# A long-convolution and MLP block on one core: ssm_k loaded and transposed in halves, PSUM places in another order, column means and the w2 load moved

## The chip, the core and the metric

The kernel runs on one core of one Trainium2 chip. The metric is the device time of one execution in microseconds (us), the median of several runs; less is better. The engines are named as in the profile: PE (TensorE, matmul), PEld (its weight loads), DVE (VectorE), ACT (ScalarE), POOL (GpSimd), SP (SyncE, which here only issues DMAs).

## The reference

S = 2048 tokens, D = 512 channels, Dff = 1376, batch 1, all inputs bf16.

```
k_shift[t] = sum over j<4 of k[t-j] * shift_k[:, j]        # per channel
kv = k_shift * v
y  = causal convolution of kv with ssm_k along t (by FFT of length 2S) + kv * ssm_D
h  = x + layernorm(x) * y            # x = A_q
h2 = h + relu(layernorm(h) @ w1) @ w2
```

## The kernel before, in words

One function writes the whole program; the schedule is manual, so each engine runs its instructions in the order of the text, and semaphores follow from what tiles are read and written. PSUM has eight banks; pools of it are opened and closed (`push`, `pop`), and a pool that is opened where another was waits for the last readers of what lay there.

The convolution is done as a Fourier transform in two steps, t being split into 32 and 64.

- **Start.** SP loads `sk` (ssm_k, 2 MB, L96), then k and v in four chunks each with transposing DMAs (L107 to L112). ACT issues the small load of `wsh` (L98). DVE and ACT build the tables of sines; `cc_turns` (two DVE instructions, L211 and L181) prepares half of one cosine table, `cc_part` (ACT, L185) finishes it. POOL builds `wdiag` (diagonal matrices of the four taps, L226), the small tables `f1hi`, `f1lo` (L228 to L230), and `f2hi`, `f2lo` (L234), which hold f1 on a block diagonal, then `c2n` (L237).
- **Transposes of ssm_k** (`to_rows`, L260): for each q of 8, eight PE transposes of 128 x 128 into one PSUM bank, then a copy to `kfl` by DVE or ACT in turn.
- **The loop over gb = 0 to 7** (L332): `taps` (L320) does the shifted sum for a chunk of k as eight matmuls into two tap banks and multiplies by v on DVE (L327; the result overwrites `sk`). `stage1` (L267) is the first transform step for 8 channel groups: either four 32-row tiles with f1, or, with `pairs`, two 64-row tiles with f2; its results are copied to `a1k` by ACT and DVE.
- **PSUM places.** `place` (L249) hands out three places of two banks in turn; after the tap banks are given back a fourth is appended (L340).
- **Transposes of kv** (L359 to L371), the second step for the kernel's transform (`ps2k`, L377), stage 1 for kv (L390), then 16 **products** (L408): `stage2` into `u`, a complex product with `kf` on DVE and POOL (L421), and `finish` (L426), which adds the parts on PE (`psy`) and copies back into `kf`. `finish` runs two products behind, the last two after the loop (L457).
- **Inverse.** `inv1` (L547), 16 blocks b, goes from `kf` to `ax` by ACT copies (DVE for b = 4, 9, 14). Between the blocks stand the layer norm of x and the centring of w1: `column_means(n)` (L528, four matmuls into a `pm` bank) for a quarter of w1's columns and a subtraction on DVE (n = 0, 1) or, after a DVE copy, on POOL (n = 2, 3). `inv2` (L606) gives y for half a token quarter in `pz`; `gate` (L596) makes h of it and has it transposed back by an SP DMA. `lift` and `ln1_norm` issue transposing DMAs of x and of its norm on SP.
- **MLP**, four token quarters: `mlp1` (L621, relu on ACT) and `mlp2` (L634). Hooks place the remaining `inv2` halves and two sine tables between its blocks. ACT issues the load of `w2` right after the inverse loop (L589, L591); it lies where `kf` was.

Of the kernel before, what the change touches and what calls it, by code (L numbers as in the profile page):

```python
# [15 lines left out]
P = 128  # L16
# [40 lines left out]
def kernel(  # L57
# [38 lines left out]
    nc.sync.dma_start(out=sk[:], in_=A_ssm_k.rearrange("(c p) t -> p c t", p=P))  # L96
# [120 lines left out]

    f1hi = early.tile([P, 64], BF16, name="f1_hi")
# [9 lines left out]
    nc.gpsimd.tensor_copy(out=f1hi[:, 0:64], in_=f1f[:])  # L228
    nc.gpsimd.tensor_tensor(out=f1f[:], in0=f1f[:], in1=f1hi[:, 0:64], op=ALU.subtract)
    nc.gpsimd.tensor_copy(out=f1lo[:, 0:64], in_=f1f[:])  # L230
# [16 lines left out]
    turn = [0]  # L247

    def place(shape, dtype, name):  # L249
        i = turn[0] % len(places)  # L250
        turn[0] += 1
        return places[i].tile(shape, dtype, tag=f"ps{i}", name=name)
# [7 lines left out]
    def to_rows(src, q, fl, eng):  # L260
        shape = [P, 8, P]
        pst = tap_bank(q % 5 - 3, shape, BF16, "pst") if q % 5 > 2 else place(shape, BF16, "pst")
        for i in range(8):
            nc.tensor.transpose(out=pst[:, i, :], in_=src[:, :, :, 8 * q + i], identity=ident[:])  # L264
        copy(eng, fl[:, :, :, 8 * q:8 * q + 8], pst[:].rearrange("p i (d g) -> p g d i", d=2))

    def stage1(fl, a_out, gb, engs, pairs=False):  # L267

        pss = [bank2("ps1") for _ in range(2)]
        n, tabs = (2, (f2hi, f2lo)) if pairs else (4, (f1hi, f1lo))  # L270
        K = P // n
        for gi in range(8):
            for f in range(2):
                for t in range(n):
                    rows = slice(K * t, K * t + K)
                    if pairs:
                        o = pss[t][:, gi // 4, 128 * (gi % 4):128 * (gi % 4) + 128]
                    else:
                        o = pss[t // 2][:, t % 2, 64 * gi:64 * gi + 64]
                    nc.tensor.matmul(out=o, lhsT=fl[rows, 8 * gb + gi, :, :].rearrange("p d n -> p (d n)"),  # L280
                                     rhs=tabs[f][rows, :], start=(f == 0), stop=(f == 1),
                                     tile_position=(K * t, 0), skip_group_check=True)
        for h in range(2):
            if pairs:
                src = pss[h][:].rearrange("p b (g r c) -> p c (b g) r", g=4, r=2)
            else:
                src = pss[h][:].rearrange("p r (g c) -> p c g r", c=64)
            dst = a_out[:, :, 32 * gb:32 * gb + 32].rearrange("p c (g r) -> p c g r", r=DC)[:, :, :, 2 * h:2 * h + 2]
            for g, eng in enumerate(engs[h]):
                n = 8 // len(engs[h])  # L290
                copy(eng, dst[:, :, g * n:g * n + n], src[:, :, g * n:g * n + n])
# [13 lines left out]
    skv = sk[:].rearrange("p c (a b) -> p c a b", b=64)  # L305
    for q in range(8):
        to_rows(skv, q, kfl, "DADADADA"[q])
    cc_turns(0)
# [23 lines left out]
    for gb in range(8):  # L332
        taps(gb // 2, gb % 2)
        if gb == 0:
            cc_turns(16)
        stage1(kfl, a1k, gb, ("AA", "AD")[gb % 2], pairs=(gb == 2))
# [3 lines left out]
    places.append(pl.push("psX", space=PSUM))  # L340
    for dp, pq in enumerate(halves):
# [48 lines left out]
    for gb in range(8):  # L390
        stage1(xfl, a1x, gb, ("A", "DA" if gb == 4 else "D"), pairs=True)
# [6 lines left out]
    psum = pl.push("psP", bufs=2, space=PSUM)  # L398
# [9 lines left out]
    def product(kp):  # L408
# [3 lines left out]
        for s in range(2):  # L412
            u = psum.tile([P, 2, 256], F32, tag=f"u{s}", name=f"u{s}")
# [12 lines left out]
    def finish(at):  # L426
        kp, (tr, ti) = pending.pop(0)
        for s, (a, b, m) in enumerate(((tr[:, 0], ti[:, 1], ineg), (tr[:, 1], ti[:, 0], ipos))):
            psy = psum.tile([P, 512], F32, tag=f"psy{s}", name=f"psy{s}")
# [26 lines left out]
    load_x(3)  # L456
    while pending:  # L457
        finish(16)
    pl.pop("psP")
# [16 lines left out]
    places[:] = [pl.push("psI", space=PSUM)] * 3  # L476
    turn[0] = 0
    psum1 = pl.push("psC", bufs=2, space=PSUM)
# [46 lines left out]
    FS = 344  # L525
    cen = {}

    def column_means(n):  # L528
        cen[n] = psum1.tile([P, 512], F32, tag="pm", name="pm")
        for c in range(DC):  # L530
            nc.tensor.matmul(out=cen[n][:, 0:FS], lhsT=ones[:], rhs=w1[:, c, n * FS:(n + 1) * FS],
                             start=(c == 0), stop=(c == DC - 1))

# [6 lines left out]

    ec_turns(0)
    ln1_stats(0)
    ec_turns(1)
    column_means(0)
    column_means(1)
# [14 lines left out]
    for b in range(16):  # L560
# [14 lines left out]
        if b == 13:  # L575
            column_means(3)
        if b in (11, 14):
            n = 2 + (b - 11) // 3
            nc.vector.tensor_copy(out=wm[:, n - 2, :], in_=cen[n][:, 0:FS])
            center(nc.gpsimd, n, wm[:, n - 2, :])  # L580
# [7 lines left out]
    nfull = DFF // P  # L588
    nc.scalar.dma_start(out=w2[:, 0:nfull, :], in_=B_w2[0:nfull * P, :].rearrange("(c p) d -> p c d", p=P))  # L589
    if DFF % P:  # L590
        nc.scalar.dma_start(out=w2[0:DFF % P, nfull, :], in_=B_w2[nfull * P:DFF, :])  # L591
# [65 lines left out]

    pl.pop("psC")
    pl.pop("psI")
# [13 lines left out]

    def in_mlp1_0(fc):
        if fc in (6, 8):
            ec_sins(2 + (fc - 6) // 2)
# [68 lines left out]
```

## Time and profile before

| | us |
|---|---|
| median of 3 runs (216.83 to 219.06) | 218.42 |
| the profiled execution, its own time | 216.73 |
| its span in the profile | 215.0 |
| PE busy | 195.1 (91%) |
| DVE, ACT, POOL busy | 144.2, 116.6, 79.6 |
| `sk` load, issue to landing | 8.2 |
| 64 transposes of `sk` (L264), busy | 6.5 |
| MLP matmuls (L628 and L645), busy | 78.2 |

The granted PE clock is 0.998 of full speed over the whole span. The DMA engines moved 20.06 MB; the transposing DMAs on SP's queue make up most of the packets. In the table and below, a start is counted from the span's start. A group line of the profile gives line, engine, operation, what is written and read, the count, busy time, the mean of one, and the idle time ahead of it with what ended it.

### The profile page before, as it was taken

The numbers are of one execution on the slowest core, as the hardware profiler recorded it, in microseconds if no ns is written. First come the engines' busy times: TensorE is split into PE (matmuls) and PEld (weight loads), VectorE is DVE, ScalarE is ACT, GpSimd is POOL, SyncE is SP. The second block draws the span as 40 slices with busy tenths as digits, with TensorE's granted clock in tenths as the row PEclk, the third lists the DMA queues.
The fourth block names the chain that finished last, engine by engine and source line by source line (L and its number), as shares of the span: only waits on it lengthen the run. The fifth ranks groups of instructions, "written<-read, shape, count | busy, mean of one in ns | idle before, by whom it ended". The sixth has DMA issues, their size and how long they took to land.

```text
span 215.0 us, 5414 instructions
## 1 busy us (share of the span) xinstructions
PE 195.1 (91%) x2235; PEld 137.3 (64%) x2235; DVE 144.2 (67%) x238; ACT 116.6 (54%) x178; POOL 79.6 (37%) x120
## 2 busy tenths in 40 slices
PE   0398998999996999998997999999999999999992
PEld 0394554999875899986997954664646644444451
DVE  7589778776796999988495993968395460243031
ACT  2967788655796788883996048202450047016400
POOL 3299993000003999995747702200201010002000
PEclk9999999999999999999999999999999999999999
DMA  6999960000000007709850897787353430020012
GB/s 192 314 219 182 159 137 6 2 2 3 0 3 5 0 3 195 262 8 212 173 98 3 265 168 129 88 184 100 76 105 68 92 82 0 15 63 23 0 50 49
DMA packets 49512, 20.06 MB, mean 93 GB/s; under 512 B 44400, under 2 KB 47952, under 8 KB 49488
## 3 DMA queue, kind: packets, MB, share of 16 engines
q1 hardware_dynamic: 47360, 18.24, 42.8%
q10 hardware_dynamic: 2128, 1.48, 2.3%
q8 instruction: 17, 0.28, 0.6%
q14 instruction: 7, 0.06, 0.1%
HBM read 7.08 MB, written 2.10 MB: 43 GB/s over the span
## 4 chain that ended last, share of the span: by engine, by line
PE 79%; DVE 7%; ACT 5%; DMA 5%; issue 1%; SPq 0%; ACTq 0%
PE ps2m L645 18%; PE ps1m L628 18%; PE pz L616 7%; PE pkv L324 6%; PE psy L431 6%; DMA sk<-in_A_ssm_k_dram 4%; PE ps L280 4%; PE ps2k L300 3%; PE ps2k L298 3%; PE u L298 3%; PE u L300 3%; PE pst L264 3%; PE psi L552 3%; ACT ax L242 2%; PE pst L362 2%; ACT a1x L242 2%
## 5 line engine op out<-in xcount | busy, mean ns | idle before, releaser
L630 ACT ACTIVATE h1T<-ps1m 128x512 bf16<-128x512 f32 (+1 forms) x44 | 26.0, 596 | 55.6 <-PE ps1m L628 55.6
L645 PE MATMUL ps2m<-w,h1T 128*128 128x512 bf16 (+3 forms) x187 | 39.4, 367 | 0.0
L628 PE MATMUL ps1m<-xT,w 128*128 128x512 bf16 (+1 forms) x176 | 38.8, 379 | 0.0
L648 DVE SCALAR_TENSOR_TENSOR o<-ps2m,rstd,xh 128x512 bf16<-128x512 f32 (+1 forms) x17 | 12.2, 719 | 32.1 <-PE ps2m L645 29.8
L628 PEld LDWEIGHTS <-w 128*128 128x128 bf16 (+1 forms) x176 | 17.5, 100 | 20.1
L645 PEld LDWEIGHTS <-h1T 128*128 128x128 bf16 (+1 forms) x187 | 17.9, 98 | 19.2
L421 POOL TENSOR_TENSOR t<-usb,kf 128x320 fp32r<-128x320 f32 x32 | 28.2, 930 | 2.4 <-ACT usb L417 2.0
L421 DVE TENSOR_TENSOR t<-u,kf 128x704 fp32r<-128x704 f32 x32 | 26.7, 889 | 3.4 <-ACT usb L417 3.4
L502 POOL TENSOR_SCALAR rstd<-mv 128x4 f32<-128x4 f32 x8 | 2.3, 283 | 67.6 <-DVE mv L500 67.6
L498 DVE BATCH_NORM_STATS2 st<-xh 128x6 f32<-128x512 bf16 x32 | 19.7, 678 | 0.0
L242 ACT CAST kf<-psy 128x512 fp32r<-128x512 f32 x30 | 17.6, 645 | 1.9 <-PE psy L431 0.3
L616 PEld LDWEIGHTS pz<-ecore,ax 32*128 32x128 f32 x512 | 15.2, 186 | 3.8 <-issue 2.1
L616 PE MATMUL pz<-ecore,ax 32*128 32x128 f32 (+7 forms) x512 | 16.1, 273 | 1.3 <-ACT ax L242 1.1
L598 DVE TENSOR_TENSOR qT<-pz,qT 128x1024 bf16<-128x1024 f32 x8 | 9.8, 1222 | 10.2 <-PE pz L616 6.7
L324 PE MATMUL pkv<-kT,wdiag 128*128 128x512 bf16 x64 | 15.2, 380 | 0.9 <-DVE sk L327 0.9
L431 PE MATMUL psy<-t,ipos 128*128 128x512 f32 x48 | 16.0, 393 | 0.0
L552 PE MATMUL psi<-dre,kf 128*128 128x256 f32 x64 | 15.5, 286 | 0.0
L552 PE MATMUL psi<-dim,kf 128*128 128x256 f32 x64 | 15.2, 280 | 0.0
L242 ACT CAST a1k<-ps 128x1024 fp32r<-128x1024 f32 x12 | 12.6, 1093 | 4.3 <-PE ps L280 4.3
L242 ACT CAST ax<-psi 128x1024 fp32r<-128x1024 f32 x13 | 12.4, 1017 | 4.6 <-DVE st L498 3.0
L264 PE MATMUL pst<-ident,sk 128*128 128x128 bf16 x64 | 6.5, 285 | 8.9 <-DMA sk<-in_A_ssm_k_dram 8.9
L327 DVE TENSOR_TENSOR sk<-pkv,vT 128x512 bf16<-128x512 f32 x16 | 10.6, 685 | 3.5 <-PE pkv L324 3.5
(116 smaller groups left out, 391.2 us busy)
## 6 DMA issues: line engine op xcount, KB each, us to landing
sk<-in_A_ssm_k_dram SPq DMA_DIRECT2D x1, 2048.0 KB, 8.2
xh<-in_A_q_dram SPq DMA_DIRECT2D x16, 128.0 KB, 3.0
out_dram<-o SPq DMA_DIRECT2D x60, 32.0 KB, 1.6
w<-in_B_w_dram SPq DMA_DIRECT2D x1, 1376.0 KB, 6.1
w<-in_B_w_dram ACTq DMA_DIRECT2D x1, 1280.0 KB
xh<-xT SPq DMA_TRANSPOSE x8, 3.6
w<-in_B_w_dram ACTq DMA_DIRECT2D x1, 96.0 KB, 8.2
kT<-in_A_k_dram SPq DMA_TRANSPOSE x4, 7.2
```

What stands on the lines that cost most here:

```text
L242: nc.scalar.copy(out=o, in_=i)
L264: nc.tensor.transpose(out=pst[:, i, :], in_=src[:, :, :, 8 * q + i], identity=ident[:])
L298: nc.tensor.matmul(out=ps[:, kk, :], lhsT=at_k1(w_re, k1), rhs=a_in[:, k1, :], start=True, stop=False, skip_group_check=True)
L324: nc.tensor.matmul(out=pss[i][:], lhsT=wdiag[:, 2 * h + i, j, :], rhs=kT[c][:, 2 * h + i, 16 - j:CH + 16 - j], start=(j == 0), stop=(j == ...
L421: eng.tensor_tensor(out=t[:, :, j, :], in0=in0.unsqueeze(1).to_broadcast([P, 2, n, 2]), in1=kfr[:, :, j, ks], op=ALU.mult)
L431: nc.tensor.matmul(out=psy[:], lhsT=m_[:], rhs=t_.rearrange("p j k -> p (j k)"), start=first, stop=not first)
L498: nc.vector.bn_stats(out=st[:, i, :], in_=src[:, i, :])
L552: nc.tensor.matmul(out=ps[:, i // 2, i % 2, :], lhsT=kf[:, c, 4 * m:4 * m + 4, :].rearrange("p r k -> p (r k)"), rhs=d[:].rearrange("p d a ...
L616: nc.tensor.matmul(out=pz[:, rg, 32 * jl:32 * (jl + w)], lhsT=ax[rows, 64 * rho + n2, :, :].rearrange("p d g -> p (d g)"), rhs=ecore[q][ro ...
L628: nc.tensor.matmul(out=ps1[:fsz, :].rearrange("p (i t) -> p i t", i=4), lhsT=w1[:, c, fc * P:fc * P + fsz], rhs=hT[sc][:, :, c, :], start= ...
L630: nc.scalar.activation(out=h1T[:fsz, fc, :], in_=ps1[:fsz, :], func=ACT.Relu)
L645: nc.tensor.matmul(out=ps2[:, 0:w], lhsT=h1T[:ksz, fc, i * P:(i + 1) * P], rhs=w2[:ksz, fc, ds], start=(fc == 0), stop=(fc == NFC - 1))
```

## The change

`sk` comes in two loads of two channel blocks each. Its transposes are 128 instead of 64, each of 64 columns into one half of the PSUM partitions: all of the first half, then all of the second, in eight banks at once; the eight copies follow. `cc_turns(0)` is issued ahead of the copies and `cc_turns(16)` after the taps of group 2 instead of group 0. Stage 1 takes its small tables from the f2 tiles in every group; in the first stage 1 groups 2, 3 and 4 are in 64-row form (before: 2), in the second all but group 0 (before: all). POOL makes `f1hi` and `f1lo` between the second and the third `wdiag`. The places follow a list that is set to 1, 3, 2, 0 once the fourth exists. The products' PSUM pool is split in two (`psU`, `psY`); the mean banks and one place of the inverse stage are opened where `psU` was, the first two column means come right after the last product, and the fourth leaves the loop over b for its end. `w2` is loaded from the hook of the first `mlp1` after its second relu.

```diff
     sk = early.tile([P, DC, S], BF16, name="sk")
-    nc.sync.dma_start(out=sk[:], in_=A_ssm_k.rearrange("(c p) t -> p c t", p=P))
+    for c in range(2):
+        nc.sync.dma_start(out=sk[:, 2 * c:2 * c + 2, :], in_=A_ssm_k[2 * c * P:2 * c * P + 2 * P, :].rearrange("(c p) t -> p c t", p=P))
     wsh = consts.tile([P, DC, KS], BF16, name="wsh")
...
 
+    cc_turns(0)
+
     f1hi = early.tile([P, 64], BF16, name="f1_hi")
...
                                 in1=wsh[:, rg, :].unsqueeze(2).to_broadcast([P, KS, P]), op=ALU.mult)
-    nc.gpsimd.tensor_copy(out=f1hi[:, 0:64], in_=f1f[:])
-    nc.gpsimd.tensor_tensor(out=f1f[:], in0=f1f[:], in1=f1hi[:, 0:64], op=ALU.subtract)
-    nc.gpsimd.tensor_copy(out=f1lo[:, 0:64], in_=f1f[:])
+        if rg == 1:
+            nc.gpsimd.tensor_copy(out=f1hi[:, 0:64], in_=f1f[:])
+            nc.gpsimd.tensor_tensor(out=f1f[:], in0=f1f[:], in1=f1hi[:, 0:64], op=ALU.subtract)
+            nc.gpsimd.tensor_copy(out=f1lo[:, 0:64], in_=f1f[:])
     for f, g in ((f1hi, f2hi), (f1lo, f2lo)):
...
     places = [psum] * 3
-    turn = [0]
+    ring = [0, 1, 2]
 
     def place(shape, dtype, name):
-        i = turn[0] % len(places)
-        turn[0] += 1
+        i = ring.pop(0)
+        ring.append(i)
         return places[i].tile(shape, dtype, tag=f"ps{i}", name=name)
...
 
-    def to_rows(src, q, fl, eng):
-        shape = [P, 8, P]
-        pst = tap_bank(q % 5 - 3, shape, BF16, "pst") if q % 5 > 2 else place(shape, BF16, "pst")
-        for i in range(8):
-            nc.tensor.transpose(out=pst[:, i, :], in_=src[:, :, :, 8 * q + i], identity=ident[:])
-        copy(eng, fl[:, :, :, 8 * q:8 * q + 8], pst[:].rearrange("p i (d g) -> p g d i", d=2))
-
     def stage1(fl, a_out, gb, engs, pairs=False):
...
         pss = [bank2("ps1") for _ in range(2)]
-        n, tabs = (2, (f2hi, f2lo)) if pairs else (4, (f1hi, f1lo))
+        n, tabs = 2 if pairs else 4, (f2hi, f2lo)
         K = P // n
...
                     rows = slice(K * t, K * t + K)
+                    cols = slice(0, P)
                     if pairs:
...
                     else:
+                        cols = slice(64 * (t % 2), 64 * (t % 2) + 64)
                         o = pss[t // 2][:, t % 2, 64 * gi:64 * gi + 64]
                     nc.tensor.matmul(out=o, lhsT=fl[rows, 8 * gb + gi, :, :].rearrange("p d n -> p (d n)"),
-                                     rhs=tabs[f][rows, :], start=(f == 0), stop=(f == 1),
+                                     rhs=tabs[f][rows, cols], start=(f == 0), stop=(f == 1),
                                      tile_position=(K * t, 0), skip_group_check=True)
...
     skv = sk[:].rearrange("p c (a b) -> p c a b", b=64)
+    psts = [tap_bank(i, [P, 8, P], BF16, "pst")[:] for i in range(2)]
+    for i in range(3):
+        pair = place([P, 2, 8, P], BF16, "pst")
+        psts += [pair[:, 0], pair[:, 1]]
+    for h, rows in enumerate(halves):
+        for q in range(8):
+            for i in range(8):
+                nc.tensor.transpose(out=psts[q][rows, i, :], in_=skv[:, 2 * h:2 * h + 2, :, 8 * q + i], identity=ident[:],
+                                    tile_position=(0, 64 * h))
     for q in range(8):
-        to_rows(skv, q, kfl, "DADADADA"[q])
-    cc_turns(0)
+        copy("DA"[q % 2], kfl[:, :, :, 8 * q:8 * q + 8], psts[q].rearrange("p i (d g) -> p g d i", d=2))
     dre = consts.tile([P, 2, 2, 64], F32R, name="dre")
...
         taps(gb // 2, gb % 2)
-        if gb == 0:
+        if gb == 2:
             cc_turns(16)
-        stage1(kfl, a1k, gb, ("AA", "AD")[gb % 2], pairs=(gb == 2))
+        stage1(kfl, a1k, gb, ("AA", "AD")[gb % 2], pairs=(1 < gb < 5))
         if gb in (0, 1, 3, 5):
...
     places.append(pl.push("psX", space=PSUM))
+    ring[:] = [1, 3, 2, 0]
     for dp, pq in enumerate(halves):
...
     for gb in range(8):
-        stage1(xfl, a1x, gb, ("A", "DA" if gb == 4 else "D"), pairs=True)
+        stage1(xfl, a1x, gb, ("A", "DA" if gb == 4 else "D"), pairs=(gb > 0))
     pl.pop("psX")
...
     prod = pl.push("prod", bufs=3, side="right")
-    psum = pl.push("psP", bufs=2, space=PSUM)
+    psu = pl.push("psU", bufs=2, space=PSUM)
+    psy_ = pl.push("psY", bufs=2, side="right", space=PSUM)
     ipos = prod.tile([P, P], F32R, name="ipos", bufs=1)
...
         for s in range(2):
-            u = psum.tile([P, 2, 256], F32, tag=f"u{s}", name=f"u{s}")
+            u = psu.tile([P, 2, 256], F32, tag=f"u{s}", name=f"u{s}")
             stage2(u, a1x, kp, s)
...
         for s, (a, b, m) in enumerate(((tr[:, 0], ti[:, 1], ineg), (tr[:, 1], ti[:, 0], ipos))):
-            psy = psum.tile([P, 512], F32, tag=f"psy{s}", name=f"psy{s}")
+            psy = psy_.tile([P, 512], F32, tag=f"psy{s}", name=f"psy{s}")
             for m_, t_, first in ((ipos, a, True), (m, b, False)):
...
     load_x(3)
+    pl.pop("psU")
+    psum1 = pl.push("psC", space=PSUM)
+    psum_a = pl.push("psIa", space=PSUM)
+    FS = 344
+    cen = {}
+
+    def column_means(n):
+        cen[n] = psum1.tile([P, 512], F32, tag=f"pm{n % 2}", name="pm")
+        for c in range(DC):
+            nc.tensor.matmul(out=cen[n][:, 0:FS], lhsT=ones[:], rhs=w1[:, c, n * FS:(n + 1) * FS],
+                             start=(c == 0), stop=(c == DC - 1))
+
     while pending:
         finish(16)
-    pl.pop("psP")
+    column_means(0)
+    column_means(1)
+    pl.pop("psY")
+    places[:] = [psum_a] + [pl.push("psIb", side="right", space=PSUM)] * 2
+    ring[:] = [0, 1, 2]
     pl.pop("prod")
...
     act_pool = {0: late, 1: late}
-    places[:] = [pl.push("psI", space=PSUM)] * 3
-    turn[0] = 0
-    psum1 = pl.push("psC", bufs=2, space=PSUM)
 
...
 
-    FS = 344
-    cen = {}
-
-    def column_means(n):
-        cen[n] = psum1.tile([P, 512], F32, tag="pm", name="pm")
-        for c in range(DC):
-            nc.tensor.matmul(out=cen[n][:, 0:FS], lhsT=ones[:], rhs=w1[:, c, n * FS:(n + 1) * FS],
-                             start=(c == 0), stop=(c == DC - 1))
-
     def center(eng, n, mean):
...
 
+    def off_center(n):
+        nc.vector.tensor_copy(out=wm[:, n - 2, :], in_=cen[n][:, 0:FS])
+        center(nc.gpsimd, n, wm[:, n - 2, :])
+
     ec_turns(0)
...
     ec_turns(1)
-    column_means(0)
-    column_means(1)
 
...
             column_means(2)
-        if b == 13:
-            column_means(3)
-        if b in (11, 14):
-            n = 2 + (b - 11) // 3
-            nc.vector.tensor_copy(out=wm[:, n - 2, :], in_=cen[n][:, 0:FS])
-            center(nc.gpsimd, n, wm[:, n - 2, :])
+        if b == 11:
+            off_center(2)
+    column_means(3)
+    off_center(3)
     ln1_stats(1)
...
     w2 = mp.tile([P, NFC, D], BF16, name="w2")
-    nfull = DFF // P
-    nc.scalar.dma_start(out=w2[:, 0:nfull, :], in_=B_w2[0:nfull * P, :].rearrange("(c p) d -> p c d", p=P))
-    if DFF % P:
-        nc.scalar.dma_start(out=w2[0:DFF % P, nfull, :], in_=B_w2[nfull * P:DFF, :])
     hT = {}
...
 
+    pl.pop("psIa")
     pl.pop("psC")
-    pl.pop("psI")
+    pl.pop("psIb")
     psz = pl.push("psZ", space=PSUM)
...
 
+    def load_w2():
+        nfull = DFF // P
+        nc.scalar.dma_start(out=w2[:, 0:nfull, :], in_=B_w2[0:nfull * P, :].rearrange("(c p) d -> p c d", p=P))
+        if DFF % P:
+            nc.scalar.dma_start(out=w2[0:DFF % P, nfull, :], in_=B_w2[nfull * P:DFF, :])
+
     def in_mlp1_0(fc):
+        if fc == 1:
+            load_w2()
         if fc in (6, 8):
...
```

## The prediction

> **What bounds the kernel now.** I read the page first (shares by engine), then the chain of work that ended last, then the timeline of each of the three places that the change touches. PE is busy 91% of the span and 79% of the chain, at a granted clock of 0.998; from 124.5 us to 211 us the chain is PE without a gap, and nothing in the change alters that MLP part except the arrival of `w2`. So a gain can only come from the places ahead of 124.5 us where PE waits. The chain shows them (start us, duration us, what):
>
> ```profile
> 0.72 8.18 DMA sk<-in_A_ssm_k_dram
> 8.95 6.49 PE pst L264 x64
> 15.44 1.74 PE pkv L324 x8
> 17.24 1.28 DVE sk L327 x2
> 18.52 0.61 DVE w_tc L211
> 19.15 1.40 DVE w_tc L181
> 20.55 0.60 DVE sk L327
> 21.20 1.89 PE pkv L324 x8
> ...
> 36.68 1.06 ACT a1k L242
> 37.83 3.88 PE pst L362 x32
> ...
> 114.53 0.60 PE pm L531 x4
> 115.13 1.92 PE psi L552 x16
> 117.07 1.02 ACT ax L242
> 118.14 4.06 PE pz L616 x127
> ```
>
> To be seen: 8.2 us of load with PE idle, then 64 transposes on the path; the two `w_tc` instructions on DVE ahead of a tap product; a wait for an ACT eviction before the second transposes; a column mean inside the inverse stage and 1.1 us of PE waiting for ACT behind it. Two timelines add what the chain hides (POOL at the start; PE after the products):
>
> ```profile
> 9.24 4.06 POOL L226 TENSOR_TENSOR wdiag<-ident,wsh 128x512 bf16<-128x512 bf16 x4 [6.07 <-DMA wsh<-in_A_shift_k_dram]
> 15.26 1.43 POOL L234 COPY f_lo<-f_lo 32x64 bf16<-32x64 bf16 x4
> ```
> ```profile
> 99.20 1.34 PE L531 MATMUL pm<-w,ones 128*128 128x344 bf16 x8 [0.84 <-DVE kf L244]
> ```
>
> POOL starts only when `wsh` lands (9.24) and finishes the padded table `f2lo` at 16.69. The column means wait 0.84 us because every PSUM buffer of the products must be free first.
>
> **What the Trainium skill says.** "TensorEngine Tiling (Array Packing)", Restrictions: column tiling disables Fast Weight Load. "TensorE: Matmul & The Clock Gate", LDWEIGHTS: a load's time goes with its columns, not its rows; the trace agrees on rows (32x128 load 92 ns, 64x128 load 94 ns). The strided 128-column load from `sk` takes 188 ns against 98 for the dense `wdiag`, so it may already be a slow load. "DMA: Bandwidth & Descriptors", Queues, rings and completion order: an engine goes round between its queues packet by packet. From 4 to 5 us the trace has 99 packets on SP's queue and 98 on ACT's, which agrees.
>
> **The change, part by part.**
>
> *Two loads, 128 narrow transposes.* SP issues one more DMA (0.47 us), all behind a running transfer. By the 1 us windows 1.05 MB of `sk` has moved by 5.4 us and all 2.1 MB by 8.05; PE started 0.9 us after that, so half one is usable at 6.3 us. Then 64 transposes of 64 columns start there and 64 more follow. A 128-column pair now costs 6.25/63 = 99 ns. No row shows the narrow one: if its cost goes with the loaded columns it is about 50 ns plus, with the moving 128 columns as the other limit; the two-row-tile stage 1 pairs with the same 128 moving columns take 1.12/16 = 70 ns. If the narrow load costs as much as the wide one it is 99 ns. I take 50 to 70: all transposes end at 6.3 + 128 x 0.06 = 14.0 (13 to 15.3) instead of 15.3; with 99 at 19.0. The evacuations (4 x 1.22 on DVE, 4 x 1.02 on ACT) can begin at about 10.6 and end at about 15.5 (before: 16.5). Taps then end at about 16.
>
> *But stage 1 of group 0 now reads `f2hi` and `f2lo`*, ready at 16.69. Moving the three `f1` instructions (0.8 us) between `wdiag` 1 and 2 changes no sum: POOL still has 4.06 + 0.8 + 2.5 us after 9.24, and `wsh` can't land sooner, as its packets alternate with the same 512 rows of `sk`. Stage 1 so starts at 16.8 instead of 17.10: -0.3, whatever the 2 us of early transposes promise.
>
> *The tap loop.* `cc_turns(0)` (1.4 us) moves into DVE's idle time at 8.1 to 10; `cc_turns(16)` (1.4 to 2.1) goes behind group 2, where DVE has 4.0 us of work in 5.9. PE's two waits for DVE (0.2 and 0.72, at 17.97 and 21.20) go: -0.9. Two more groups in 64-row form cost 1.12 - 0.62 each: +1.0. With ACT a little late for group 2 (its first copies and the 1.27 us table come first) I add 0.3, half of it in parallel: +0.15. Without cover I see nothing that hides the +1.0. The loop ends at 36.5 - 0.3 - 0.9 + 1.0 + 0.15 = 36.45; the sum is about 0 to -0.4, and I use -0.3. The transposed k and v must not be overtaken: the last v chunk is issued at 25.55 and takes 5.4 us (31.0), its user runs at 32.95, so 2 us of lead is all that is left there.
>
> *Free order of PSUM places.* The second transposes start at 37.83 because their first place is the one that ACT evacuates at 36.66 to 37.73. In the order 1, 3, 2, 0 they start when the last tap product is written (36.71): -1.1 there. DVE is busy until 37.93 with the other eviction, so the last four are held: redoing the eight by 0.485 us each, with copies of 0.69 and 1.2, the last ends at 40.7 instead of 41.44: -0.75.
>
> *Group 0 of the x stage in 32-row form.* PE saves 0.5, but the stage is paced by ACT: its last `kf` copy ends at 57.28, and 8 copies of 1.12 and a half follow. 0.
>
> *Means behind the products.* `psC` and the first inverse place lie in the banks of `psU`, whose last reader is done at 97.2; PE goes from the last product (98.36) straight into the 8 mean matmuls (1.04) and the inverse stage starts at 99.45 instead of 100.24, just after DVE's last `kf` write at 99.14: -0.8. `column_means(3)` (0.6) leaves the loop and runs while ACT does its last `ax` copy: the loop ends 1.4 us earlier (115.6), ACT's copy at 116.7, and `pz` starts at 116.8 instead of 118.14: -1.35. Behind the moved mean stand on DVE its 0.5 us copy (116.25 to 116.75), the second statistics (2.8), and both gates (1.9 each): they end at 123.3, where PE's own three `pz` halves end at 123.05. MLP starts at 123.4 instead of 124.5: -1.1. POOL's subtraction (2.84) ends at 119.6, 4 us before its use.
>
> *w2 late.* The two DMAs move from 117.1 to ACT's second relu, 1.95 us after MLP start M. Queued behind them on ACT: relu 2 and on, 0.27 us of idle time in each, and four PSUM buffers; nothing. `w2` is first read at M + 9.5. Before, its second part landed 8.2 us after issue; `w1`, of the same size, 6.1. Uncontended: M + 8.1 to M + 9.8. But SP's transposes of x and q run from M + 1.2 to M + 6 and land at about M + 8.5; alternating with 1 KB packets (50 ns against about 20) stretches the 4.4 us of transfer to 6.2, so M + 10.7 at worst in this count. Wait: 0 to 1.2; I take +0.4, since half of the first transpose is over by then. Cover gone: a late qT delays the gate that the next `pz` half waits for; it has 2.2 us to spare.
>
> **Sum** against the span of 215.0 (216.73 with what lies around it): -0.3 - 0.75 - 1.1 + 0.4 = -1.75, near 215.0 for such an execution. The median shown is 218.42, 1.7 above the profiled one; the same difference gives 216.7. I go to 216.5, since the stage 1 wait may give 0.2 more.
>
> **Rivals.**
> - *w2 stalls PE* (chance 0.20). PE has no other work between the two MLP halves. If the transposes take half of each engine, 1.4 MB needs 8 us: landing at M + 12, wait 2.0 to 2.5 in place of 0.4, and the late gate adds up to 0.6. 216.5 + 2 = 218.5. For it: both queues share 16 engines that are saturated from 126 to 132 (share 1.06). Against: `w1` moved at 340 GB/s alone.
> - *The narrow transposes cost as much as wide ones* (0.12), the slower end. At 99 ns each they end at 19.0, taps at 20.8, stage 1 at 20.9: +3.8 in place of -0.3, so 216.5 + 4.1 = 220.6. It decides from 83 ns: 6.3 + 128 x 0.083 + 1.9 = 18.8 is where the other gains (1.75) are eaten. For it: twice as many instructions on the same columns moved; against: loads go with columns.
> - *More than counted* (0.18): the POOL chain ends sooner, and the tap loop is paced by ACT (18.2 us of copies and tables) so that the 64-row groups cost nothing. Then -1.5 more: 215.0.
>
> **How the numbers follow.** The counted case has 0.50, with its own range 215.4 to 217.8. About 1% (2.2 us) is what a measurement of this kernel can tell from no change. Faster by more (under 216.2): 0.28 of the counted case and the 0.18, together 0.46. Within: 0.22, 0.18 of the w2 rival and 0.03, 0.43. Slower: 0.11. The range leaves out the far half of the slow rival and the best few per cent: 214.0 to 219.6.
>
> **What would show it.** First narrow transpose at 6.3 and last before 15; stage 1's first matmul at POOL's last `f_lo` copy; second transposes one us after the last tap stage without an ACT wait; no gap between products and means; `pz` right behind ACT's last `ax`; MLP start about 2.2 us sooner; at the first `ps2m`, either no wait or one for the `w` DMA. I am wrong if PE waits there for over 1 us, if the transposes pace at over 83 ns, or if POOL is no longer last ahead of stage 1.

## The result, and the profile after

The changed kernel takes 223.90 us (median of 4 runs, 223.60 to 224.41) where the kernel before took 217.79 beside it (4 runs, 216.83 to 219.06): a ratio of 1.028, 95% interval 1.022 to 1.034. The forecast of 216.5 and its range are both missed; the kernel became 6.1 us slower. The profiled execution has a time of 223.77 us and a span of 222.0 (before: 215.0). The ratios, here and below, leave out executions more than 1.5% above the fastest of the same kernel, and the medians don't, so the two need not agree to the last digit.

The same marks on PE in both profiles (the first start of each kind of matmul, in us; the tap loop is taken to the end of its last stage 1 matmul) show where the 7.0 us of span lie:

| stretch | before | after | difference | forecast |
|---|---|---|---|---|
| span's start to first stage 1 matmul | 17.10 | 22.60 | +5.50 | -0.3, with the next row |
| tap loop, first stage 1 matmul to the end of the last | 19.50 | 19.09 | -0.41 | |
| loop's end to first `ps2k` | 4.87 | 3.93 | -0.94 | -0.75 |
| `ps2k` to first `u` | 25.80 | 26.20 | +0.40 | 0 |
| `u` to MLP start | 57.23 | 55.81 | -1.42 | -1.1 |
| MLP start to the `pz` behind the first `ps2m` | 11.97 | 15.45 | +3.48 | +0.4 |
| from there to the span's end | 78.53 | 78.92 | +0.39 | 0 |

So the middle of the kernel did roughly what was forecast, and both ends did not. The chain of work that ended last, after, at the kernel's start:

```profile
0.72 5.42 DMA sk<-in_A_ssm_k_dram
...
6.18 14.07 PE pst L312 x128
...
20.27 1.24 DVE kfl L248
...
21.53 1.02 ACT kfl L246
...
22.60 0.72 PE ps L279 x64
```

The first half of `sk` is usable at 6.18, as forecast (6.3), but the 128 narrow transposes take 14.07 us, 110 ns each, where 64 wide ones took 6.49. Behind them two copies stand one after the other, DVE's and then ACT's; in the kernel before such copies overlapped. The waits of ACT after (total, times, longest) say the same:

```profile
ACT kfl L246 <- DVE kfl L248: 3.6, 3, 2.0
```

POOL, forecast as the last ahead of stage 1, is long done (its timeline after):

```profile
6.45 2.04 POOL L229 TENSOR_TENSOR wdiag<-ident,wsh 128x512 bf16<-128x512 bf16 x2 [3.28 <-DMA wsh<-in_A_shift_k_dram]
14.87 1.09 POOL L238 COPY f_lo<-f_lo 32x64 bf16<-32x64 bf16 x4
```

The timeline of PE after, in the middle: the second transposes follow the tap loop at 0.26 us and wait for DVE, not for ACT's eviction, and the means have no wait ahead of them (before: 0.84).

```profile
41.95 3.88 PE L370 MATMUL pst<-ident,sk 128*128 128x128 f32 x32 [0.26 <-DVE sk L334]
102.73 1.34 PE L475 MATMUL pm<-w,ones 128*128 128x344 bf16 x8
```

At the MLP, the waits of PE after (total, times, longest) and the DMA view's count of packets from 132 to 133 us (then MB and their share of the engines' time; q10 is ACT's queue with `w2`, q1 is SP's with the transposes of x and q):

```profile
PE ps2m L654 <- DMA w<-in_B_w_dram: 2.9, 1, 2.9
PE pz L625 <- DVE qT L607: 0.4, 1, 0.4
```
```profile
q10 hardware_dynamic: 226, 0.23, 79.8%
q1 hardware_dynamic: 232, 0.06, 33.4%
```

PE stands still for 2.9 us until `w2` is there. The two queues share the engines one packet for one packet (226 against 232; in the next two windows of 1 us 275 against 271 and 278 against 285), although a packet of `w2` carries 1 KB and one of the transposes 256 B. ACT issues the load at 129.57; its packets begin at 131.7 and end near 140, and on SP's side the last transpose of q lands 10.8 us after its issue, so the gate and the next `pz` are late too.

Taking turns is not all of it. At 275 packets a microsecond the 1408 packets of `w2` would need 5.1 us, and at the 353 to 370 that they reach alone in e3 (below) about 3.9 (estimates from these counts); they took 8.1. Part of the rest is standstill: between 135.5 and 135.9 and between 137.2 and 138.4 next to no packet starts on either queue, and the packets of `w2` that start at 137.1 take 1.4 us each, against 46 ns at the median. From 137 to 138:

```profile
q10 hardware_dynamic: 42, 0.04, 115.6%
q1 hardware_dynamic: 49, 0.01, 65.0%
```

Packets of over 1.3 us occur on SP's queue in the profile of every kernel here, also where `w2` isn't moving (at 125 us in e5, at 133 in e2 below). What holds the DMA engines then stays open.

### The profile page after: what moved, and what is told of

It reads as the page before. It is cut to its first block, busy times and chain, and to the rows that moved or that the text cites. A ratio compares the mean times of both kernels' runs of the same rounds, so it can differ in the third digit from the quotient of the medians.

```text
span 222.0 us, 5464 instructions
## 1 busy us (share of the span) xinstructions
PE 202.5 (91%) x2253; PEld 145.1 (65%) x2267; DVE 145.2 (65%) x238; ACT 116.1 (52%) x178; POOL 79.4 (36%) x120
## 4 chain that ended last, share of the span: by engine, by line
PE 73%; DVE 10%; DMA 8%; ACT 4%; issue 2%; SPq 1%; DVEq 0%; ACTq 0%
PE ps2m L654 14%; PE ps1m L637 13%; PE psy L440 7%; PE pst L312 6%; PE pkv L331 6%; DMA qT<-qln 5%; PE ps L279 5%; PE pz L625 4%; PE ps2k L297 3%; PE ps2k L299 3%; PE u L297 3%; PE psi L567 3%; PE u L299 3%; DMA sk<-in_A_ssm_k_dram 2%; PE pst L370 2%
## 5 line engine op out<-in xcount | busy, mean ns | idle before, releaser
L654 PE MATMUL ps2m<-w,h1T 128*128 128x512 bf16 (+2 forms) x179 | 38.7, 366 | 3.5 <-DMA w<-in_B_w_dram 2.9
L312 PE MATMUL pst<-ident,sk 128*64 128x128 bf16 x128 | 14.1, 292 | 6.2 <-DMA sk<-in_A_ssm_k_dram 6.2
L312 PEld LDWEIGHTS <-sk 128*64 128x64 bf16 x128 | 13.9, 204 | 6.2 <-DMA sk<-in_A_ssm_k_dram 6.2
## 6 DMA issues: line engine op xcount, KB each, us to landing
w<-in_B_w_dram ACTq DMA_DIRECT2D x1, 1280.0 KB, 10.6
```

The costliest lines, as they stand in the source:

```text
L312: nc.tensor.transpose(out=psts[q][rows, i, :], in_=skv[:, 2 * h:2 * h + 2, :, 8 * q + i], identity=ident[:], tile_position=(0, 64 * h))
L654: nc.tensor.matmul(out=ps2[:, 0:w], lhsT=h1T[:ksz, fc, i * P:(i + 1) * P], rhs=w2[:ksz, fc, ds], start=(fc == 0), stop=(fc == NFC - 1))
```

## Experiments

Times are medians in us; "before" is the kernel before, run beside each on the same chip. The kernel before read between 216.76 and 217.79 in the course of them, so differences from the changed kernel, which was run at another time, carry up to 1 us of that: the 5.8, 3.9 and 7.5 us of e1, e2 and e3 below are 5.5, 3.6 and 7.2 when each kernel is taken against the kernel before beside it. In several of these kernels the executions fall into two groups some 2 us apart, the upper with a granted clock near 0.99, and medians mix them; what lies behind is told with the third experiment.

| kernel | time | before | ratio, 95% interval |
|---|---|---|---|
| changed kernel | 223.90 | 217.79 | 1.028 (1.022 to 1.034) |
| e1, wide transposes | 218.13 | 217.48 | 1.003 (1.001 to 1.006) |
| e2, `w2` early | 220.04 | 217.48 | 1.011 (1.009 to 1.014) |
| e3, both | 216.41 | 217.48 | 0.997 (0.994 to 0.999) |
| e4, before with `w2` late | 219.18 | 216.99 | 1.011 (1.007 to 1.015) |
| e5, e3 with tiles of its own | 216.39 | 216.99 | 0.996 (0.992 to 1.000) |
| e6, e5 with `w2` in two | 214.73 | 216.99 | 0.989 (0.984 to 0.993) |
| e7, alternating transposes | 220.48 | 216.99 | one run |
| e8, e6 with one 64-row group | 216.98 | 217.26 | 0.998 (0.995 to 1.001) |
| e9, e6 with the old place order | 216.07 | 217.26 | 0.996 (0.993 to 0.998) |
| e10, e6 with the fourth mean inside | 215.57 | 217.26 | 0.995 (0.992 to 0.998) |
| e11, e6 once more | 215.26 | 216.76 | 0.993 (0.991 to 0.996) |

**e1: the wide transposes put back.** The two loads, the eight banks and all else stay.

```diff
-    for h, rows in enumerate(halves):
-        for q in range(8):
-            for i in range(8):
-                nc.tensor.transpose(out=psts[q][rows, i, :], in_=skv[:, 2 * h:2 * h + 2, :, 8 * q + i], identity=ident[:],
-                                    tile_position=(0, 64 * h))
+    for q in range(8):
+        for i in range(8):
+            nc.tensor.transpose(out=psts[q][:, i, :], in_=skv[:, :, :, 8 * q + i], identity=ident[:])
```

> The changed kernel with the 128 narrow transposes put back to 64 wide ones (128 columns, into the same eight banks, both loads kept); all else as changed. Theory (each narrow transpose costs as much PE time as a wide one, about 109 ns, so the block takes 14.1 us in place of 6.4): transposes end near 15.3 us instead of 20.25, the first stage 1 moves from 22.6 to about 17.5, and the time falls by 4.5 to 5.5 us, to about 219. Rival (stage 1 of group 0 is held by the padded f2 table on POOL and by the copies of two places that share one tile, not by the transposes): the time falls by less than 2.5 us.

Measured: 5.8 us less than the changed kernel. Stage 1 starts at 17.76 instead of 22.60. The narrow transposes are the larger part of the loss.

**e2: `w2` loaded behind the inverse loop again**, narrow transposes kept.

```diff
     w2 = mp.tile([P, NFC, D], BF16, name="w2")
+    load_w2()
...
-        if fc == 1:
-            load_w2()
```

> The changed kernel with the load of w2 put back behind the inverse loop; all else as changed. Theory (w2 and the transposing DMAs of x and q share the 16 DMA engines packet by packet, so w2 takes 10.6 us to land and the q transpose 10.8; PE waits 2.9 us for the one and about 0.9 for the other): both waits go, the time falls by 3 to 4 us, to about 220.3. Rival (PE would stand at the first ps2m for something else, or the late gate alone sets the pace): it falls by less than 1.5 us.

Measured: 3.9 us less than the changed kernel. PE waits for no DMA at `ps2m`; from the first `ps1m` to the first `ps2m` it takes 9.50 us, as in the kernel before (9.50), where the changed kernel took 12.55.

**e3: both.**

> The changed kernel with both put back: wide transposes and w2 behind the inverse loop. Theory (the two costs are at different places and add; what remains of the change, the order of places and the means behind the products, is worth about 2.3 us): 8 to 9 us less than the changed kernel, about 215.3, 1% less than the kernel before. Rival (the remaining edits are hidden or paid back by the two additional 64-row groups): equal to the kernel before within 0.5%.

Measured: 216.41, 1.1 above the expectation, 7.5 below the changed kernel. Its 20 runs fall into 11 at 215.57 to 216.63 (clock 0.996 and more) and 9 at 217.54 to 219.12 (clock 0.984 to 0.991). The profile caught one of the latter. Its timeline of PE and its 1 us windows (the number after the busy shares is the clock, then the DMA share and GB/s):

```profile
116.19 5.01 PE L630 MATMUL pz<-ecore,ax 32*128 32x256 f32 x162 [0.70 <-DVE wm L553]
123.35 2.07 PE L630 MATMUL pz<-ecore,ax 32*128 32x256 f32 x30 [2.15 <-issue]
```
```profile
122.00:123.00 1.00, 0.00 (x0) 0.00 (x0) 1.00 (x4) 0.00 (x0) 0.00 (x0) 1.00 1.25 182
123.00:124.00 1.00, 0.65 (x12) 0.65 (x16) 1.00 (x5) 0.00 (x0) 0.00 (x0) 0.68 0.47 97
124.00:125.00 1.00, 1.00 (x24) 1.00 (x22) 1.00 (x5) 0.00 (x0) 0.00 (x0) 0.50 1.12 192
125.00:126.00 1.00, 1.00 (x10) 0.41 (x5) 1.00 (x3) 0.00 (x0) 0.00 (x0) 0.50 2.31 159
126.00:127.00 1.00, 1.00 (x4) 0.38 (x3) 1.00 (x3) 0.00 (x0) 0.00 (x0) 0.61 0.13 7
```

PE stands still for 2.15 us with nothing that the profile shows to wait for ("issue"), and then its clock is at half from 123.3 to 126.8. From `pz` to the MLP start it takes 9.17 us, 6.27 in e1, and 0.7 more is lost behind it. That is 3.6 us, more than the 2.2 between the medians of the two groups, so the lower group may hold a part of the stop as well (no profile of it was taken). It accounts for part of the difference between e1's gain and e2's (together 9.6) and e3's (7.5): from the lower group's median, 215.94, e3's gain is 8.0.

**Six orders of transposes**, to price the narrow one: the 128 transposes of the changed kernel are replaced by six runs of 32. In turn: strided columns of 64 in one column tile, consecutive columns of 64 in one column tile, strided with the column tiles in turn, consecutive with the column tiles in turn, strided columns of 128, consecutive columns of 128.

```diff
+    for q in range(4):
+        for i in range(8):
+            nc.tensor.transpose(out=psts[q][lo, i, :], in_=skv[:, 0:2, :, 8 * q + i], identity=ident[:], tile_position=(0, 0))
+    for q in range(4):
+        for i in range(8):
+            nc.tensor.transpose(out=psts[q][lo, i, :], in_=sk[:, i % 4, 64 * (8 * q + i):64 * (8 * q + i) + 64], identity=ident[:], tile_position=(0, 0))
...
```

> A measurement of the transposes by themselves: the block of transposes of the changed kernel is replaced by six runs of 32, one after the other: narrow (64 columns) with a stride of 64 elements in one column tile; narrow and dense in one column tile; narrow strided with the two column tiles in turn; narrow dense in turn; wide strided; wide dense. The output isn't the reference's, since the transposed data are others. Theory A (the load of 64 columns costs what one of 128 does, since the narrow form loads slowly): about 109 ns each in all four narrow runs, 99 for wide strided, less for wide dense. Theory B (inside one column tile the next load waits for the matmul before it): about 109 in one tile, about 55 to 70 in turn. Theory C (the stride is what costs): about 109 strided, under 80 dense, in narrow and wide alike.

Measured in a single execution, of which only this stretch is used, by the timeline of PE:

```profile
6.11 3.79 PE L311 MATMUL pst<-ident,sk 128*64 128x128 bf16 x32 [6.11 <-DMA sk<-in_A_ssm_k_dram]
9.73 1.84 PE L314 MATMUL pst<-ident,sk 128*64 128x128 bf16 x30
...
11.52 2.13 PE L318 MATMUL pst<-ident,sk 128*64 128x128 bf16 x31
13.37 1.17 PE L322 MATMUL pst<-ident,sk 128*64 128x128 bf16 x32
14.47 3.09 PE L325 MATMUL pst<-ident,sk 128*128 128x128 bf16 x32
17.40 1.95 PE L328 MATMUL pst<-ident,sk 128*128 128x128 bf16 x32
19.19 1.03 PE L346 MATMUL pkv<-kT,wdiag 128*128 128x512 bf16 x4
```

From start to start, divided by 32: 113 ns (strided, one column tile), 56 (consecutive), 58 (strided, in turn), 34 (consecutive, in turn), 92 (wide, strided), 56 (wide, consecutive). The two that matter by their weight loads:

```profile
L311 PEld LDWEIGHTS <-sk x32: 187/206/208, 6.1 to 9.6; 128*64 128x64 bf16 x32
L325 PEld LDWEIGHTS <-sk x32: 168/203/217, 14.5 to 17.2; 128*128 128x128 bf16 x32
```

A strided load of 64 columns takes 206 ns at the median, one of 128 columns 203: half the columns save nothing. The stride doubles both (consecutive: 110 and 98). So none of the three theories holds alone: a consecutive narrow load isn't dear (against A), and a strided one is dear only behind another on the same column tile (B and C together). The 50 to 70 ns of the forecast is what consecutive columns cost, or strided ones whose neighbours go to the other column tile.

The clock has to be kept apart from this. The records of the granted clock begin only at 9.7 us in this run, at 12.0 in the changed kernel and at 12.6 in the kernel before; the 0.998 in the table of the kernel before takes the time ahead of them as full speed. At these times the matmuls get shorter (317 to 275 ns in the changed kernel), and the wide transposes of the kernel before go from 107 ns each to 91. The narrow strided ones stay at 110 to 113 ns, and their loads at 203 to 207, on both sides of 12.0. So the first of the six runs, which lies ahead of 9.7, may be compared with the fifth; and the 99 ns that the prediction read for a wide transpose is a mean of 107 and 91, so behind 12 us the narrow form costs 110 to 112 against 91.

**e7: that last point in the kernel.** The loop over the two column tiles becomes the innermost one; every pair then needs both loads.

```diff
-    for h, rows in enumerate(halves):
-        for q in range(8):
-            for i in range(8):
+    for q in range(8):
+        for i in range(8):
+            for h, rows in enumerate(halves):
```

> The changed kernel with the loop over the two column tiles innermost, so that each 64-column transpose is followed by one on the other column tile; all of them now wait for the second load (8.8 us). Theory (a strided 64-column load takes 110 ns behind another on the same column tile, and 65 ns when the column tiles alternate, as in the run with six orders): 128 x 65 ns, so transposes from 8.8 to 17.1 and the first tap at 17.2 instead of 20.2, stage 1 near 20.5 and 1.5 to 2.5 us less than the changed kernel. Rival (a 64-column load simply costs what a 128-column load costs, 99 ns or more): 128 x 99 to 110 ns, transposes until 21.5 to 22.9, 1.3 to 2.7 us slower than the changed kernel.

```profile
6.05 0.37 PE L312 MATMUL pst<-ident,sk 128*64 128x128 bf16 x1 [6.05 <-DMA sk<-in_A_ssm_k_dram]
8.72 8.05 PE L312 MATMUL pst<-ident,sk 128*64 128x128 bf16 x127 [2.30 <-DMA sk<-in_A_ssm_k_dram]
16.70 1.47 PE L331 MATMUL pkv<-kT,wdiag 128*128 128x512 bf16 x5
```

Measured: 63 ns each, the first tap at 16.70 (expected 17.2), 3.4 us less than the changed kernel although all but the first start 2.5 us later. The same 128 instructions in another order take 8.0 us in place of 14.0, so the cost is in two strided loads to one column tile in a row, not in the number of instructions. It is still behind the wide form (15.3). The total is from one execution, in which PE also stopped for 2.18 us ahead of `ps2m` and then ran at half clock; the start of the profile is what counts here.

**e4: the kernel before with `w2` late, and nothing else.** The issue moves from behind the inverse loop into the hook, as in the change's diff.

> The kernel before, with its w2 load alone moved to the second relu of the first MLP. Theory of contention (w2 alternates packet by packet with SP's transposes and so lands 10 to 11 us after its issue, where it lands in 6 when the queues are free): first MLP product at about 124.3, w2 issued at about 126.6, landing at about 137, while the second MLP's product wants it at 134: 3 us of PE wait at ps2m, and 0.4 to 0.7 more from the late q transposes; 3.0 to 3.7 us above before. Rival, as it was forecast: a load off the critical path, a gain of 0.2 against a wait of under 0.6, so 217.4 to 218.2.

Measured: 2.2 us more than before. The large part lands 9.3 us after its issue; first `ps1m` to first `ps2m` takes 11.26 us (before 9.50), from there to the next `pz` 3.07 (2.47): 2.4 together. The wait is there without any other part of the change, so the rival falls; it is 1 us smaller than in the changed kernel, as the load lands 1.3 us sooner, and the expected 3.0 to 3.7 was too much.

The landing time is the cause: the DMA issues of the changed kernel and then of e3 (engine, count, size, median us to landing).

```profile
w<-in_B_w_dram ACTq DMA_DIRECT2D x1, 1280.0 KB, 10.6
```
```profile
w<-in_B_w_dram ACTq DMA_DIRECT2D x1, 1280.0 KB, 6.3
```

With the queues free the load takes 6.3 us here, 6.6 in e2 and 7.8 in e5, and 129.57 + 6.3 to 7.8 = 135.9 to 137.4 would have been ahead of the product's place at 137.1 (127.63 + 9.50) or 0.3 behind it. Beside SP's transposes it takes 9.3 to 10.6 (e4, e1, the changed kernel); its first packet then starts 2.0 to 2.1 us after the issue, not 1.05.

**e5: one PSUM tile for each eight transposes**, on top of e3: `to_rows` of the kernel before comes back.

```diff
-    psts = [tap_bank(i, [P, 8, P], BF16, "pst")[:] for i in range(2)]
-    for i in range(3):
-        pair = place([P, 2, 8, P], BF16, "pst")
-        psts += [pair[:, 0], pair[:, 1]]
...
+        to_rows(skv, q, kfl, "DADADADA"[q])
```

> The changed kernel with wide transposes, w2 behind the inverse loop, and the loop of the kernel before that gives each group of eight transposes a PSUM tile of its own (so five tiles in turn instead of eight at once). Theory of the shared tile (two halves of one two-bank tile make DVE's copy wait for the transposes of both, and ACT's for DVE's copy): DVE and ACT copy side by side again, the flattened kernel is ready by 16.6, and stage 1 starts behind the taps at 17.1 to 17.2 instead of 17.9: 0.7 us below the run with the shared tiles (216.4 median of its runs). Rival (POOL's last table copy ends at 15.9, or the taps themselves, hold stage 1): no difference, within 0.2 us.

PE's timelines, e3 and then e5:

```profile
17.91 0.21 PE L279 MATMUL ps<-f_hi,kfl 32*128 32x64 bf16 x4 [0.64 <-ACT kfl L246]
```
```profile
17.15 0.21 PE L286 MATMUL ps<-f_hi,kfl 32*128 32x64 bf16 x4
```

Stage 1 starts at 17.15 without a wait, as expected. e3 has the contrast within itself: its first two copies, whose tiles are banks of their own, overlap (from 10.87 on DVE, from 10.78 on ACT), and each of ACT's other three waits for DVE's on the other half of the tile; in e5 none does. In the median nothing of the 0.7 us is seen: the two groups are there again (7 of 12 runs at 215.14 to 216.94, 5 at 217.51 to 218.14), and its profile lost 0.5 us in `ps2k`, where e6, which has the same instructions there, did not.

**e6: `w2` in two**, on top of e5: 640 KB behind the inverse loop, 736 KB in the hook.

```diff
-    load_w2()
+    nc.scalar.dma_start(out=w2[:, 0:5, :], in_=B_w2[0:5 * P, :].rearrange("(c p) d -> p c d", p=P))
...
+        if fc == 1:
+            load_w2()
```

Its `load_w2` now loads the rows from 5 * P on.

> As the run with tiles of its own, with w2 in two: its first five blocks of 128 rows (640 KB) behind the inverse loop, the rest (736 KB) at the second relu of the first MLP. Theory (what costs is that 1376 KB share the rings with SP's transposes for all of the second MLP's lead): the late half needs about 5.5 us for its contended packets and lands near 132, before or within 0.5 us of the second MLP's first product, so that no wait of over 0.5 us at ps2m is left; and the early half is through within 3 us, so that PE's idle stretch inside the second inverse transform (2.2 us in the run with both undone, with a TensorE clock of half for 3.4 us behind it, in about half of its runs) does not come: 0.3 to 1.0 us below the run with tiles of its own, with nearly all runs at one level. Rival (that stretch has nothing to do with w2's load): two levels of runs some 2 us apart as before, and a median the same within 0.3 or up to 1 us more from the late q transposes.

```profile
121.74 9.67 PE L641 MATMUL ps1m<-xT,w 128*128 128x512 bf16 x44
131.24 2.54 PE L658 MATMUL ps2m<-w,h1T 128*128 128x512 bf16 x10
134.11 1.96 PE L629 MATMUL pz<-ecore,ax 32*128 32x128 f32 x64 [0.33 <-DVE qT L611]
```

Measured: no wait for `w2`, 0.33 us for the late q, `pz` without a stop (6.27 us to the MLP start), 214.73.

**e8, e9, e10: three parts of the change undone in e6**, one in each: `pairs=(gb == 2)`; `ring[:] = [2, 3, 0, 1]`, which is the order of the kernel before at that place; the fourth mean back at b = 13 and 14.

> The kernel with w2 in two, with only group 2 of stage 1 in 64-row form (as in the kernel before) in place of groups 2, 3 and 4. Theory as forecast (the 64-row form costs PE 0.5 us more per group, since 1.12 stands against 0.62 in the profile of before, and nothing hides it): the tap loop is 1.0 us shorter (18.2 instead of 19.2 us from its first stage 1 matmul to its last) and the time about 214.0 against 214.7. Rival (64-row groups are evacuated in another pattern and spare a wait; or the loop is paced by ACT's and DVE's copies, so that the form costs PE nothing): the loop takes 18.9 to 19.5 us and the time stays within 0.4 of 214.7.

Measured: the loop takes 18.65 us; in e6 it took 19.17, in e11 19.32, in the other kernels with three such groups 19.00 to 19.41 (but 20.18 in e10, which stopped there for 0.95, see the end). Two 64-row groups cost 0.35 to 0.75, between theory and rival. The time does not show it: 11 of 20 runs are in the upper group, after a wait of 1.51 us for q in the profile.

> The kernel with w2 in two, with the PSUM places behind the tap loop taken in the order of the kernel before (2, 3, 0, 1) in place of 1, 3, 2, 0. Theory: the second transposes wait for ACT's eviction of the place that they are to use, 0.7 to 1.1 us between the loop's last matmul and the first transpose instead of 0.25; the u stage starts 0.5 to 0.9 us later, and the time is 215.2 to 215.6. Rival (the second transposes are paced by DVE's and ACT's own evictions, so that the order gives nothing in the end): u within 0.2 us of 65.8, time within 0.3 of 214.7.

```profile
PE pst L368 <- ACT a1k L246: 1.3, 1, 1.3
```

Measured: ACT's eviction is awaited again (1.28 us between loop and transposes, 0.25 in e6), `u` starts at 67.01 against 65.81 in e6, of which 0.24 is the loop. The order is worth about 0.95; the runs of the lower group have a median of 215.87, 0.6 to 1.1 above e11 and e6.

> The kernel with w2 in two, with the fourth column mean and its subtraction back inside the inverse loop (at steps 13 and 14, as in the kernel before) in place of behind it. Theory: 0.6 us of PE in the loop, so the inverse stage ends 0.6 us later, and pz follows 1.1 us behind it, ACT's last eviction between them: pz starts 0.3 to 0.6 us later than 97.8 + 17.65 and the MLP with it; 215.0 to 215.3. Rival (the gate chain on DVE sets the MLP's start, and its mean copy stands sooner inside the loop): MLP start within 0.2 us, time within 0.3 of 214.7.

```profile
116.57 1.69 PE L629 MATMUL pz<-ecore,ax 32*128 32x256 f32 x48 [1.10 <-ACT ax L246]
```

Measured: from the first mean to the MLP start 25.20 us, against 24.98 and 24.92 in e6 and e11. Moving the fourth mean is worth 0.2 to 0.3; the theory's lower edge.

> The kernel with w2 in two once more, since its median (214.73) stands on four runs, while three kernels next to it had a second level some 2 us up in 2 of 12, 5 of 20 and 11 of 20 runs. If that level comes from PE's idle time of 1.5 us or more ahead of the second MLP (late q transposes) and not from the kernel's form, this kernel has it too: a few of its runs near 217, the rest at 214.4 to 215.4, a median of 214.8 to 215.5 and a ratio of 0.989 to 0.993. If the level needs what the three others changed, all runs stay below 215.8.

Measured: 215.26, one of 11 runs (217.03) at a clock of 0.992. e6's form beats both kernels, by 0.7% of the kernel before with e11's interval, about 1.5 us, and the changed kernel by about 7.6 (6.1 and 1.5, each against the kernel before beside it).

## Why the prediction was wrong, step by step

- **"I take 50 to 70" ns for a narrow transpose: the step that failed.** It measured 110, with the price argued from columns loaded and from stage 1 matmuls whose weights aren't strided. The rival "cost as much as wide ones" put it at 99 and 220.6, with a chance of 0.12; even that was under the measured price. The prediction held the clue and passed over it: the strided 128-column load at 188 ns (a mean; 203 at the median from 13 us on) against 98 for a dense one. "TensorE: Matmul & The Clock Gate", Step-by-step: what each phase is for, has load time scale with the column count; for the loads here that does not hold (strided 206 ns at 64 columns, 203 at 128; consecutive 110 and 98). e1 returns 5.8 us, the six orders give the price, e7 shows what in it can be avoided.
- **w2 late, "+0.4": right mechanism, mis-sized.** The wait was 2.9 and the late q cost 0.4 to 0.6 more, 3.5 in all; e2 returned 3.9. The count "M + 10.7 at worst" took 6.2 us for the contended transfer, where the packets ran for 8.1 us, from 131.7 to near 140; its own M + 9.8, stretched by 1.8, would already have been M + 11.6. The counts (226 to 232) show one reason: the queue of small packets takes as many turns as that of large ones for as long as both have work. The later first packet (1 us) and the standstills at 135.5 and 137.2 (about 1.6 together) were in no count. The rival's 8 us of transfer, M + 12 and wait of 2.0 to 2.5 us were nearly right (8.1, M + 12.5, 2.9), in part by luck: turns alone make 5.1 us, and the standstills weren't in its count either.
- **"`wsh` can't land sooner": wrong, without consequence.** It landed 5.6 us after its issue, at 6.31, just behind the first half of `sk` (6.14); POOL started at 6.45 (before 9.24) and was done with `f_lo` at 15.96, so that the table never held stage 1. Had the transposes been free, the shared PSUM tiles would have: 0.6 to 0.8 us (e3 against e5), a wait that the prediction did not have.
- **Tap loop.** Forecast +0.25 over the loop, measured -0.41. The two DVE waits went as forecast, the 64-row groups cost 0.2 to 0.4 each in place of 0.5 (e8).
- **Place order, -0.75: right.** -0.94 in the profiles, about -0.95 by e9. It is worth less where PE itself is late there: e4, in the old order, waited 0.49 in place of 1.24, behind a stop of PE of 0.52.
- **x stage, 0:** `ps2k` to `u` +0.40, but e5 and e6 differ there by 0.55 with the same instructions, so it says nothing.
- **Means, -1.1: right in sum** (-1.42), not in its parts: the move ahead of the inverse stage gave 1.0 (forecast 0.8), the fourth mean 0.2 to 0.4 (forecast 0.3 net).
- **Sum.** -0.41 - 0.94 - 1.42 = -2.8 against a forecast of -2.15 for all but `w2` (which has -0.3 for start and loop together, where the prediction's own terms, 36.5 to 36.45, make -0.05); with the wide transposes and an uncontended `w2` this is what e6 shows (span 212.6 against 215.0). The loss is 5.5 at the start and 3.5 at the MLP; 0.8 of the span's 7.0 is in the two stretches for which 0 was forecast.

## What to carry to other kernels

Before a wide operation is cut into narrow ones, price the narrow one with its own access pattern: here a strided weight load took as long for half the columns (206 ns against 203), and only the order (neighbours on different column tiles) gave some of it back. A load with slack by its landing time alone can lose that slack when another queue with many small packets runs beside it (6.3 to 7.8 us became 9.3 to 10.6); move it in parts, into the stretch where the queues are free. Where two engines evacuated halves of one PSUM tile they ran one after the other (e3), and with a tile for each they overlapped (e5), so give each its own.

## What else the runs showed

- Narrow transposes of consecutive columns, with the column tiles in turn, run at 34 ns, against 56 in one column tile or at full width: two column tiles work side by side.
- **A short stop of PE can cost twice.** In the profiles of e3, e5, e7 and e8, PE idled for 2.15, 1.9, 2.18 and 1.51 us and then ran at half clock for about 3.4 us, losing 1.7 us more. In the changed kernel 2.87 and in e1 2.07 us of waiting had no such sequel. "TensorE: Matmul & The Clock Gate", What's actually happening, tells of a free-running window of 3.4 us after which an idle array goes to half clock; the length of the slow stretch agrees, and in each trace all changes of the clock lie on a grid of 3.41 us counted from the first one (in e3 109.23 us behind it, 32 steps, in e8 122.88, 36 steps). But here idle times shorter than a window were enough, in some executions, and how much PE idled within one step of that grid doesn't decide: 1.1 us in e8, 1.5 in e5 and 2.2 in e3 and e7 were followed by half clock, 1.9 in the changed kernel and 1.5 at the first `u` of most kernels here were not. In e3, e5 and e8 the 32-row matmuls of `pz` stand next to the stop; whether that is what tells them apart, no run here shows.
- What PE waited for from 121.2 us in e3 and from 120.9 in e5 stays open: the profile names nothing. At that place it appeared only with all of `w2` moving just ahead of it, and in none of the five profiles with `w2` in two nor in those with it late. But e2 and the kernel before move all of `w2` there too and show no such stop (at most 0.2 us), and stops without a named releaser occur where no `w2` moves: 0.52 us in e4 at 36.4, and 0.95 in e10, in the tap loop. So the load of `w2` is not shown to be their cause. The stop of e10:

```profile
23.11 0.23 PE L286 MATMUL ps<-f_lo,kfl 64*128 64x128 bf16 x2 [0.95 <-issue]
```
